# Softmax weights in a PSUM bank, more of the attention's additions open to GpSimd, and a new order, in a two-layer mixer kernel

## The chip, the cores and the metric

The kernel runs on one core of one Trainium2 chip. A core has five engines with queues of their own: TensorE (PE, matrix products; its weight loads are shown as PEld), VectorE (DVE), ScalarE (ACT), GpSimd (POOL) and SyncE (SP, which here issues the DMAs). They work side by side and wait for one another by semaphores. Data lie in SBUF (128 partitions), and matrix products land in PSUM, which this kernel uses as eight banks of 128 x 512 float32. The metric is device time in microseconds (us) of one execution; lower is better.

## The reference

x is 2048 rows of 512 float32. Two kinds of layers follow each other twice: x + A(layernorm(x)), then x + B(layernorm(x)). B (not touched by the change) is two layernorms, a spatial shift between two 512 x 512 products, and an MLP of 512 x 1792 and 1792 x 512 with gelu. A is attention with 32 heads of 16 numbers in which each row sees itself and seven earlier rows, two apart:

```python
idx = pos[:, None] - off[None, :]          # off = 0, 2, ..., 14
mask = idx >= 0
logits = jnp.einsum("bhsd,bhswd->bhsw", q, kg) * scale     # kg, vg: rows idx of k and v
logits = jnp.where(mask[None, None, :, :], logits, -1e9)
attn = _softmax(logits, axis=-1)
o = jnp.einsum("bhsw,bhswd->bhsd", attn, vg)
```

The kernel scales and shifts the logits by the maximum of the eight, takes exp, divides by the sum and adds up eight products for each output number. It must give these numbers whichever engine does a step.

## The kernel before, in words

The 2048 rows are cut into four blocks of 512 rows; with two layer pairs there are eight blocks n = 0 to 7. For each block the stages are: `p1_stream` (block 0: `p1_quarters`) normalizes x and makes q, k and v; `p2` is the attention; `p3` multiplies by wo, adds the residual and makes h; `p4` multiplies by w2; `p5` is the MLP (blocks 6 and 7 in the form `p5_pair`). Most products of float32 matrices are made as three products of float16 halves (high times high, high times low, low times high). So the normalizing steps end in `turn_dma` (lines 696 to 716): ACT rounds the high half, DVE or GpSimd subtracts it to get the low half, and a DMA transposes both (tiles `xt` and `nT`) for PE.

The attention of a block has two units, `p2_unit`, each for two quarters of the heads (U = 2; a quarter is 8 heads, 128 columns). In a unit:

- lines 1104 to 1113: for each quarter and each pair of row tiles, DVE multiplies windows of k by q into `prod` (128 x 2048) and sums 16 numbers at a time into the logits L (128 x 512 for the unit).
- lines 1127 to 1133: maximum over the eight window places, L minus maximum, exp on ACT, sum, reciprocal, L times reciprocal, all in SBUF and all on DVE but the exp.
- lines 1145 to 1161: for each quarter and pair of tiles, a product of V's windows with the weights into `prod` (2048 numbers a partition, 2 tiles x 8 window places x 128 columns), then a tree of three additions: `add4` (1024 sums), `add2` (512) and `add1` (256, into o). `add2` and `add1` may be made by DVE or GpSimd, `add4` by DVE.

Every step is an operation of a graph (`op`, with the helpers `dve`, `act`, `gp`, `pe`, `dma`). An operation has one or more alternatives, each with its engine and a planning cost in us. Two tables written out at the head of the file set what the program does: `PLACES` gives each operation, by its number, its place in the one order in which `plan` hands the operations out, and `OTHER` lists the numbers of operations that take their second alternative, the other engine. A class `InOrder` holds each engine's instructions in this order. The word "lock" on an alternative is a mark for the planner and is not used when the program runs.

Buffers are handed out by kind, in the same order, and come back when the last operation that touches them has been passed: `prod` has one buffer (`prod0` is a second one, for block 0 only), `L` two, `mm` four PSUM banks, `acc` four PSUM banks. All groups of matmuls but the sums over the MLP's width use `mm` banks: PE fills one with (mostly) twelve matmuls, and ACT or DVE empties it.

The profile puts nearly all instructions on one line (L335, the helper that issues them), so groups are told by their tiles: `prod<-kv,q` is the product with q (in block 0 some show x for q), `L<-prod` its sum, `prod<-kv,L` the product with the weights, `prod<-prod` the first two additions, `o<-prod` the last, `L<-L,mx` the subtraction of the maximum and the multiplication by 1/sum, `small` the one-number-a-partition statistics of the layernorms.

Of the kernel before, what the change touches and what calls it, by code (L numbers as in the profile page):

```python
# [12 lines left out]
ALU = mybir.AluOpType  # L13
# [4 lines left out]
P = 128  # L18
# [4 lines left out]
NT = 4  # L23
# [3 lines left out]
H8 = 8  # L27
DH = 16
W = 8
# [22 lines left out]
PE, DVE, ACT, POOL, SP = range(5)  # L52
# [268 lines left out]
def tile_mixer(ctx, tc, x_d, wqkv_d, wo_d, w1_d, w2_d, w3_d, w4_d, out_d):  # L321
# [73 lines left out]
    op = Graph()  # L395
# [82 lines left out]
    def dve(key, d, fn, r, w, lock=False, after=()):  # L478
        return op(key, [(DVE, d, fn, "lock" if lock else None)], r, w, after)
# [576 lines left out]
    def p2_unit(n, qts):  # L1056
        op.stage = ("p2_unit", n)
        l, b = lb[n]
        U = len(qts)
        L = Buf("L")  # L1060
        LW = NT * W * H8
# [552 lines left out]
```

## Time and profile before

| what | value |
|---|---|
| median of 3 runs | 1125.81 us (1124.1 to 1126.22) |
| the profiled execution | 1125.26 us |
| its span, from the first to the last instruction | 1123.5 us |
| granted TensorE clock | 0.999 |
| PE busy | 1105.1 us, 98% of the span |
| DVE busy | 935.1 us, 83% |
| ACT busy | 656.8 us, 58% |
| POOL busy | 496.1 us, 44% |

The page gives for each engine the time in which it was busy, the span in slices, the chain of work that ended last, and groups of instructions with their busy time, the mean duration of one in ns, and the idle time ahead of them with what ended it. A busy PE is not PE at its peak, since the ends of matmuls are modelled; idle time of an engine that is not the bottleneck costs nothing. Views of the trace give the same for any stretch of the span.

### The profile page before, as it was taken

The page shows a single profiled execution, that of the slowest core. Times are in us where ns is not written, and L with a number is a line of the kernel's source. Part 1 is how long each engine was busy: PE and PEld are TensorE (multiplying, and loading weights), DVE is VectorE, ACT ScalarE, POOL GpSimd, SP SyncE. Part 2 cuts the span into 40 slices and gives each one's busy share as a digit, 9 for nine tenths or more (in the row PEclk, how much of TensorE's full clock was granted, in tenths as well). Part 3 has the DMA queues.
Part 4 walks back from the last instruction along what each step waited for, and adds up shares of the span by engine and source line. Part 5 has one row for each costly group of instructions (what it writes and reads, how often), then busy time and mean ns, then how long its engine had stood idle before and what let it go on. Part 6 is the DMA issues. An engine that isn't in the chain of part 4 may idle for free.

```text
span 1123.5 us, 16172 instructions
## 1 busy us (share of the span) xinstructions
PE 1105.1 (98%) x5488; PEld 550.8 (49%) x5488; DVE 935.1 (83%) x1062; ACT 656.8 (58%) x1242; POOL 496.1 (44%) x583
## 2 busy tenths in 40 slices
PE   8999999999999999999999999999999999999998
PEld 6544444544444444444444444444444447455764
DVE  5999999989899789879999899789887999746431
ACT  4976885358853577366655566464555654466341
POOL 4658584336531453123535345335524357333231
PEclk9999999999999999999999999999999999999999
DMA  8789999989998579946798859995889759556642
GB/s 219 193 228 223 235 267 244 265 229 230 240 241 215 127 186 209 239 125 166 172 241 201 207 126 248 248 236 164 200 211 240 198 138 251 147 155 130 186 136 61
DMA packets 268995, 224.00 MB, mean 199 GB/s; under 512 B 143688, under 2 KB 205128, under 8 KB 268912
## 3 DMA queue, kind: packets, MB, share of 16 engines
q1 hardware_dynamic: 267296, 221.20, 78.7%
q10 hardware_dynamic: 1616, 1.77, 0.6%
q8 instruction: 43, 0.70, 0.3%
q14 instruction: 40, 0.33, 0.1%
HBM read 143.65 MB, written 41.54 MB: 165 GB/s over the span
## 4 chain that ended last, share of the span: by engine, by line
PE 78%; DVE 8%; DMA 4%; POOL 3%; ACT 2%; issue 2%; SPq 1%; POOLq 0%; DVEq 0%; ACTq 0%
PE mm L335 55%; PE acc L335 23%; DVE prod L335 4%; DVE L L335 1%; POOL small L335 1%; DMA w<-in_B_w_dram 1%; SPq L335 1%; DMA out_dram<-x 1%; POOL f L335 1%; DMA w<-w 1%; ACT junk L335 0%; DVE mx L335 0%; POOL prod L335 0%; DMA xt<-f 0%; ACT f L335 0%
## 5 line engine op out<-in xcount | busy, mean ns | idle before, releaser
L335 PE MATMUL acc<-w,g 128*128 128x512 f16 (+1 forms) x1092 | 268.0, 396 | 1.4 <-DMA w<-in_B_w_dram 0.7
L335 PE MATMUL mm<-nT,w 128*128 128x512 f16 (+2 forms) x1176 | 235.8, 354 | 2.7 <-DMA nT<-f 2.7
L335 PE MATMUL mm<-wq_hl,xt 128*128 128x512 f16 x1008 | 225.3, 379 | 4.5 <-DMA xt<-f 4.0
L335 PEld LDWEIGHTS <-w 128*128 128x128 f16 x1464 | 139.5, 98 | 121.7 <-issue 6.7
L335 PEld LDWEIGHTS <-g 128*128 128x128 f16 x1176 | 114.7, 98 | 136.5 <-DVE g L335 2.1
L335 PEld LDWEIGHTS <-xt 128*128 128x128 f16 x1008 | 98.3, 98 | 122.8 <-DMA xt<-f 5.2
L335 DVE TENSOR_TENSOR prod<-kv,L 128x2048 f32<-128x2048 f32 x64 | 151.3, 2364 | 3.1 <-POOL o L335 2.1
L335 DVE TENSOR_REDUCE L<-prod 128x128 f32<-128x2048 f32 x64 | 146.1, 2283 | 1.1
L335 ACT ACTIVATE mm<-mm,s_w 128x512 f32<-128x512 f32 (+1 forms) x109 | 70.0, 645 | 117.1 <-PE mm L335 116.7
L335 DVE TENSOR_TENSOR prod<-kv,q 128x2048 f32<-128x2048 f32 x58 | 135.1, 2329 | 2.2 <-POOL o L335 0.8
L335 DVE TENSOR_TENSOR prod<-prod 128x512 f32<-128x512 f32 (+1 forms) x115 | 120.4, 1048 | 3.1
L335 POOL TENSOR_TENSOR small<-small,nhalf 128x1 f32<-128x1 f32 (+1 forms) x104 | 87.3, 842 | 64.5 <-ACT small L335 60.3
L335 POOL TENSOR_SCALAR small<-small 128x1 f32<-128x1 f32 (+1 forms) x129 | 68.5, 533 | 66.8 <-ACT junk L335 31.7
L335 POOL TENSOR_TENSOR g<-f,g 128x512 f16<-128x512 f32 x35 | 45.9, 1315 | 94.2 <-ACT f L335 49.8
L335 PE MATMUL mm<-w_hl,h 128*128 128x512 f16 x384 | 86.0, 379 | 0.0
L335 PE MATMUL mm<-nT,w_hl 128*128 128x512 f16 x384 | 85.8, 379 | 0.0
L335 PE MATMUL mm<-wo_hl,oT 128*128 128x512 f16 x336 | 74.2, 379 | 0.0
L335 ACT ACTIVATE ev<-mm,s_kv 128x512 f32<-128x512 f32 x56 | 38.0, 681 | 52.5 <-PE mm L335 32.1
L335 PEld LDWEIGHTS <-oT 128*128 128x128 f16 x426 | 41.7, 98 | 49.3
L335 POOL TENSOR_TENSOR o<-prod 128x256 f32<-128x256 f32 x26 | 22.7, 872 | 83.6 <-DVE prod L335 74.0
L335 PEld LDWEIGHTS <-w_hl 128*128 128x128 f16 x384 | 37.5, 98 | 44.9 <-issue 0.5
L335 PEld LDWEIGHTS <-h 128*128 128x128 f16 x384 | 37.6, 98 | 44.6
(250 smaller groups left out, 1585.6 us busy)
## 6 DMA issues: line engine op xcount, KB each, us to landing
w<-w SPq DMA_DIRECT2D x183, 256.0 KB
kv<-kv_d SPq DMA_DIRECT2D x112, 352.0 KB
w<-in_B_w_dram SPq DMA_DIRECT2D x56, 256.0 KB
kv_d<-ev SPq DMA_DIRECT2D x112, 128.0 KB
q_d<-ev SPq DMA_DIRECT2D x28, 256.0 KB
w<-g SPq DMA_DIRECT2D x28, 256.0 KB
q<-q_d SPq DMA_DIRECT2D x28, 256.0 KB
x<-x SPq DMA_DIRECT2D x27, 256.0 KB
```

The costliest lines, as they stand in the source:

```text
L335: i = f(*a, **k).ins
```

## The change

Three things are changed.

First, the weights (exp times 1/sum) are no longer written back into L in SBUF. The multiplication writes them to a new buffer `Lm` of kind "mm", a PSUM bank (512 float32 for the two quarters of a unit), and the four products with V of the unit read them there. These products lose their planner's mark "lock".

Second, `add4` and the subtraction of the maximum get a second alternative on GpSimd, as `add2` and `add1` had before. All handle two row tiles at a time, as before.

Third, `PLACES` and `OTHER` are written anew: another order of all 3807 operations, and 366 operations instead of 333 on their second alternative.

```diff
+        Lm = Buf("mm")
+        Lmv = lambda u: Lm.t[:, LW * u:LW * (u + 1)].rearrange("p (h t j) -> p t j h", t=NT, j=W)
...
-        dve(kd, t2, lambda: V.tensor_sub(L4(), L4(), wide(mx)), [mx], [all_L], lock=True)
+        op(kd, [(DVE, t2, lambda: V.tensor_sub(L4(), L4(), wide(mx)), "lock"),
+                (POOL, 1.95 * t2, lambda: G.tensor_sub(L4(), L4(), wide(mx)), None)], [mx], [all_L])
...
-        dve(kd, t2, lambda: V.tensor_mul(L4(), L4(), wide(sm)), [sm], [all_L], lock=True)
+        dve(kd, t2, lambda: V.tensor_mul(Lm.t[:, :U * LW].rearrange("p (h t j) -> p h t j", t=NT, j=W), L4(), wide(sm)),
+            [sm, all_L], [Lm], lock=True)
...
                 dve(kd + 0.02, 2.29, lambda i=i, pv4=pv4, kv=kv, u=u: V.tensor_tensor(
                     pv4().rearrange("p t j (h d) -> p t j h d", d=DH), win_h(kv[1].t, i, 2),
-                    Lv(u)[:, i:i + 2].unsqueeze(4).to_broadcast([P, 2, W, H8, DH]), ALU.mult),
-                    [all_L, *kv_in[1]], [pr, (o, 9)], lock=True)
+                    Lmv(u)[:, i:i + 2].unsqueeze(4).to_broadcast([P, 2, W, H8, DH]), ALU.mult),
+                    [Lm, *kv_in[1]], [pr, (o, 9)])
...
-                dve(kd + 0.01, 1.215, lambda f=add4: f(V), [], [pr], lock=True)
+                op(kd + 0.01, [(DVE, 1.215, lambda f=add4: f(V), "lock"), (POOL, 2.45, lambda f=add4: f(G), None)], [], [pr])
```

In the new order the multiplication by 1/sum of the two units of block 3 stands at places 1447 and 1615, and the last of their four products at 1661 and 1687. Between 1615 and 1661 stand PE's groups into "mm" at 1619, 1627, 1637, 1646, 1653 and 1658 and one group into "acc" at 1657, DVE's product at 1644, and at 1648 the DVE instruction that empties the bank of the group of 1637.

348 rows, old and new, of tables (OTHER, PLACES) are left out of this document.

## The prediction, written before the changed kernel ran

> **What bounds the kernel now.** I read the span first, then busy time by stage (the view of windows: busy time, instructions in brackets, then clock and DMA share), then what TensorE waited for, then the chain of waits inside the stage in which it waited.
>
> ```profile
> span 1123.5 us, 16172 instructions
> ```
> ```profile
> 0.00:25.00 25.00, 21.72 (x118) 17.17 (x119) 11.75 (x34) 10.19 (x28) 10.94 (x38) 1.00 0.87 218
> 25.00:75.00 50.00, 49.98 (x196) 26.57 (x195) 49.19 (x47) 43.06 (x107) 27.52 (x29) 1.00 0.77 206
> 75.00:200.00 125.00, 116.35 (x556) 55.92 (x555) 118.66 (x132) 88.29 (x173) 89.44 (x79) 1.00 0.97 241
> 200.00:925.00 725.00, 724.10 (x3316) 330.78 (x3315) 644.89 (x678) 425.70 (x783) 298.96 (x347) 1.00 0.83 204
> 925.00:1000.00 75.00, 73.85 (x472) 45.71 (x471) 57.77 (x75) 36.12 (x62) 35.07 (x38) 1.00 0.76 204
> 1000.00:1123.50 123.50, 119.11 (x837) 74.61 (x835) 52.87 (x100) 53.47 (x95) 34.18 (x54) 0.99 0.45 122
> ```
>
> The columns after the length are PE, PEld, DVE, ACT and POOL. PE is the bound almost everywhere: from 200 to 925 us it is idle for 725.00 - 724.10 = 0.9 us, while DVE has 80 us to spare there. The change removes no matmul, so what can be won is PE's idle time: 3.3 us at the start (nothing has arrived yet), 8.65 us from 75 to 200, 0.9, then 1.15 from 925 to 1000, and 4.4 in the last stretch (the last tiles' additions and stores after the last matmul). Start and end stay. That leaves 8.65 + 0.9 + 1.15 = 10.7 us, 1% of the span, as the most that any relief of the other engines can give. Four fifths of it lie where DVE is busy 118.66 of 125 us. PE's own waits:
>
> ```profile
> PE mm L335 <- DMA xt<-f: 4.0, 4, 1.4
> PE mm L335 <- DMA nT<-f: 2.7, 1, 2.7
> PE mm L335 <- DVE f L335: 2.2, 2, 1.4
> PE mm L335 <- ACT f L335: 1.1, 1, 1.1
> PE acc L335 <- DVE g L335: 1.1, 2, 1.0
> ...
> PE mm L335 <- DVE h L335: 0.4, 1, 0.4
> PE mm L335 <- ACT ev L335: 0.2, 1, 0.2
> ```
>
> The first two are waits for transposed tiles that the normalizing steps deliver. The last two are all that PE ever waits for a PSUM bank to be emptied: 0.6 us with four "mm" banks. Behind one of the four waits on xt (chain of waits, 103 to 120 us):
>
> ```profile
> 104.38 2.97 POOL small L335 x2
> 107.35 0.08 issue
> 107.44 3.36 POOL small L335
> ...
> 115.23 4.29 DMA xt<-f
> ```
> ```profile
> 105.32 5.74 POOL L335 TENSOR_SCALAR small<-small 128x1 f32<-128x1 f32 x3
> ```
> ```profile
> 104.96 2.29 DVE L335 TENSOR_TENSOR prod<-kv,L 128x2048 f32<-128x2048 f32 x1
> 107.29 1.22 DVE L335 TENSOR_TENSOR prod<-prod 128x1024 f32<-128x1024 f32 x1
> 108.43 2.28 DVE L335 TENSOR_TENSOR prod<-kv,L 128x2048 f32<-128x2048 f32 x1
> ```
>
> Three GpSimd instructions of one number a partition take 5.74 us, because DVE runs products of V with the weights (prod<-kv,L) beside them. With DVE on an instruction that has one operand in PSUM, this does not happen:
>
> ```profile
> 1044.05 0.42 DVE L335 TENSOR_TENSOR f<-mm,ev 128x256 f32<-128x256 f32 x1
> ```
> ```profile
> 1044.02 0.73 POOL L335 TENSOR_TENSOR f<-f,ev 128x256 f32<-128x256 f32 x1 [2.22 <-DVE f L335]
> ```
>
> There GpSimd's addition started 0.03 us before DVE's and neither held the other.
>
> **The change, part by part.**
>
> ```profile
> L335 DVE TENSOR_TENSOR prod<-kv,L 128x2048 f32<-128x2048 f32 x64 | 151.3, 2364 | 3.1 <-POOL o L335 2.1
> ...
> L335 DVE TENSOR_TENSOR prod<-prod 128x1024 f32<-128x1024 f32 x64 | 84.0, 1313 | 1.7
> L335 DVE TENSOR_TENSOR prod<-prod 128x512 f32<-128x512 f32 x51 | 36.5, 715 | 1.4
> ```
> ```profile
> L335 POOL TENSOR_TENSOR prod<-prod 128x512 f32<-128x512 f32 x14 | 20.2, 1446 | 50.8 <-DVE prod L335 50.8
> ...
> L335 POOL TENSOR_TENSOR w_hl<-nT,w_hl 128x1024 f16<-128x1024 f32 x1 | 2.1, 2138 | 0.1
> ```
>
> 1. Weights in PSUM. The 16 multiplications by 1/sum write an "mm" bank, and the 64 products read it. An operand in PSUM is priced by
>
> ```profile
> L335 DVE TENSOR_TENSOR f<-mm,ev 128x512 f32<-128x512 f32 x11 | 7.5, 683 | 12.0 <-issue 4.8 <-ACT ev L335 3.9 <-PE mm L335 3.3
> ...
> L335 DVE TENSOR_TENSOR x<-x,f 128x512 f32<-128x512 f32 x9 | 6.2, 683 | 0.1
> ```
>
> 683 ns from PSUM and 683 ns from SBUF: no price. An unhindered product took 2.28 (above) against a mean of 2.364, so up to 64 x 0.08 = 5 us of DVE time may go; writing to PSUM instead of SBUF has no row of its own, and I bound it between 0 and 0.1 us a piece (16 of them, 1.6 us), and take 0. The Trainium skill's page "VectorE: DVE Perf Modes", section "The TRN2 errata", speaks against this: its table gives a PSUM source 62 cycles more at 0.96 GHz, by which the products would take 64 x 0.065 = 4.2 us more (an estimate), a half microsecond of it among the eight products between 75 and 200 us. The two rows of 683 ns do not show it.
>
> 2. GpSimd gets more. The list OTHER names the operations that take their second engine. Counted in the order in which the program makes them: of the 64 first additions (128x1024) 8 go to GpSimd, of the 16 subtractions of the maximum 5, of the 64 second additions 18 where 13 went, of the last additions 27 where 26 went; of the 28 low halves for xt 19 where 14 went; of the residual additions 10 where 14 went. With the rows of 512 elements for subtractions, second additions and low halves, and 0.4 us on DVE and 1.1 on GpSimd for a last addition (256 elements, an estimate that continues the rows of 1024 and 512), DVE loses 8 x 1.313 + 15 x 0.715 + 0.4 = 21.6 us and gets 4 x 0.683 = 2.7 back: 19 us net. GpSimd gets 8 x 2.14 + 15 x 1.45 + 1.1 - 4 x 1.45 = 34 us. An addition of 1024 elements on GpSimd is not in the trace in this form; the row of 2138 ns has two inputs of that length and is the nearest; below it is bounded by DVE's 1.31, above by 2 x 1.446 = 2.9, which includes being held by DVE. Added wait: prod is one buffer (two in block 0), so the next product on DVE stands behind a first addition on GpSimd and the two steps after it, and whatever follows the product in DVE's queue waits too. Eight times up to 2.14 - 1.31 = 0.8 us more is 6.6 us of DVE idle at worst. From 200 to 925 DVE's 80 idle us hide it; three of the eight lie in block 0, where a second product buffer is the cover, and would cost DVE 2.5 us without it.
>
> 3. Order. PLACES is written anew. PE's sequence is nearly the old one; SP issues the same transfers, none more.
>
> What PE gains, by its waits. The wait ahead of 119.57 us loses 5 us of its chain (5.74 against about 0.75 for three free instructions) but is itself only some 0.9 us long: -0.9, after which the transfer of 4.29 us is late next. Of the other three waits on xt (3.1 us) I take away not quite half, because GpSimd now makes two more of the low halves that feed them and DVE has less ahead of them: -1.4. Of the 2.7 on nT a third: -0.9; its chain is longer and ends in a transfer. In the stage from 925 to 1000 this row of the chain of waits lies ahead of PE:
>
> ```profile
> 964.09 1.13 DVE g L335
> ```
>
> It stands behind a product with V that held GpSimd; I take half of the 1.15 us: -0.6. For the lent bank I add 0.5, about as much again as today's 0.6. Sum: -0.9 - 1.4 - 0.9 - 0.6 + 0.5 = -3.3 us. The profiled execution took 1125.26 us by the clock of the runs (span 1123.5), the median of the three runs 1125.81, 0.05% above it. Forecast: **1122.0 us**.
>
> **Rivals.**
>
> *DMA is what PE waits for.* From 75 to 200 us the 16 DMA engines are busy 0.97 of the time, and the waits on xt and nT end in transfers of 4.29 us and more. An earlier subtraction then only queues earlier. The terms on xt and nT vanish (3.2 us of the 3.3), the bank's 0.5 and the 0.6 cancel: 1125.2. Against it: ahead of the transfer the chain spends 6.3 us in GpSimd alone.
>
> *The lent bank stops PE (slower).* A bank is held from the multiplication by 1/sum to the last of four products. In block 3 the new places of two such units overlap: 1447 to 1661 and 1615 to 1687, so between 1615 and 1661 two banks are left, and PE has six groups that write "mm" there (1619, 1627, 1637, 1646, 1653, 1658) with one acc group among them. Today the same groups run back to back with all banks:
>
> ```profile
> 427.94 13.11 PE L335 MATMUL mm<-wq_hl,xt 128*128 128x512 f16 x60
> 440.89 10.52 PE L335 MATMUL mm<-nT,w 128*128 128x512 f16 x48
> ```
>
> Nine groups of twelve matmuls, 2.59 us each. The group at 1653 needs the bank that DVE empties at 1648, right behind a product at 1644: if DVE lags by one product, PE stands for 2.3 to 3 us. It decides once two or three such stalls occur over the 16 units: at half a microsecond for each unit (8 us) the time is 1125.3 - 3.8 + 8 = 1129.5. The Trainium skill's page "PSUM — Partial Sum Buffer", section "Summary: rules for kernel authors", says the same in four words, "Evacuate promptly"; no row shows what a bank held for tens of microseconds does here. For it: PE has no slack at all from 200 to 925, each stall counts in full. Against it: bank waits are 0.6 us today.
>
> *The port is not freed.* If the products go on holding GpSimd, the added 34 us of GpSimd work meet the old locks, and additions of 2.14 us hold DVE in turn: term one goes, waits grow by one or two, 1126.5. The pair of rows at 1044 us speaks against it.
>
> **How the numbers follow.** A measurement of this kernel can tell about 0.2%, 2.3 us, from no change. The forecast with its neighbours (1118 to 1123.5) gets 0.50, DMA 0.25, the bank 0.20, the port 0.05, of which I count 0.03 as the same and 0.02 as slower. So faster 0.50, same 0.28, slower 0.22. The lower end takes two thirds of the 10.7 us, with the bank free: 1117.5. The upper end takes in the bank's case: 1130.
>
> **What would show it.** Right: GpSimd's small instructions under prod<-kv products keep 0.2 to 0.6 us; the mean of those products falls to 2.28 to 2.30; idle PE from 75 to 200 falls to some 5.5 us; PE's waits on ACT and DVE that empty banks stay under 1.5 us in all. Wrong: idle PE of several microseconds between 200 and 925, released by ACT ev or by DVE g, h, x or f (the bank); idle PE from 75 to 200 as before, released by DMA (the first rival); small GpSimd instructions of 2 us beside prod<-kv products (the port).

## The result, and the profile after

The changed kernel takes 1140.72 us (median of 4 runs, 1135.84 to 1143.46) against 1126.01 of the kernel before (4 runs, 1124.1 to 1129.2): ratio 1.0125, 95% interval 1.0109 to 1.0142. It is slower, and outside the range that was forecast (1117.5 to 1130). The profiled execution took 1138.72 us. Of all executions told of here one, of the version with four units below, ran at a granted clock of 0.655 and took 1669.28 us; no ratio counts it.

The page's span and busy times, then the view of windows for three of the same stages as before, for PE alone (length, PE busy and its instructions, clock, DMA share, GB/s):

```profile
span 1136.9 us, 16149 instructions
...
PE 1108.8 (98%) x5488; PEld 551.1 (48%) x5488; DVE 907.6 (80%) x1023; ACT 646.9 (57%) x1219; POOL 505.5 (44%) x643
```
```profile
25.00:75.00 50.00, 44.45 (x170) 0.93 0.68 184
75.00:200.00 125.00, 118.04 (x560) 1.00 0.95 235
200.00:925.00 725.00, 717.55 (x3280) 1.00 0.82 203
```

DVE lost 27 us of work, as the change meant it to, and PE's idle time rose from 18.4 us (1123.5 - 1105.1) to 28.1. By stage: 25 to 75 us from 0.02 to 5.55, 75 to 200 from 8.65 down to 6.96, 200 to 925 from 0.9 to 7.45. PE's work itself is 3.7 us longer; the clock row of the first stage shows half of that (below). What PE waited for:

```profile
PE mm L337 <- ACT x L337: 5.5, 2, 5.3
PE mm L337 <- ACT junk L337: 3.9, 3, 2.0
PE mm L337 <- ACT ev L337: 3.5, 4, 1.8
PE mm L337 <- DMA nT<-f: 2.3, 3, 1.1
PE acc L337 <- POOL g L337: 1.5, 2, 0.9
PE mm L337 <- DVE f L337: 1.5, 1, 1.5
```

`ACT x` and `ACT ev` empty banks: 9.0 us where `ACT ev` had 0.2. The longest wait, at 50.19 us, stands before the first bank is lent (the first multiplication that writes one starts at 63.3 us). Three timelines of the changed kernel, of ACT, GpSimd and DVE, show how it came about (start, length, instruction, and in brackets the idle time ahead of it and its releaser):

```profile
41.67 1.89 ACT L337 ACTIVATE wo_hl<-nT 128x2048 bf16<-128x2048 f32 x1
...
43.56 0.86 ACT L337 ACTIVATE x<-mm,small 128x128 f32<-128x128 f32 x3
48.98 0.29 ACT L337 ACTIVATE small<-small 128x1 f32<-128x1 f32 x1 [4.56 <-POOL small L337]
...
49.27 1.64 ACT L337 ACTIVATE x<-mm,small 128x128 f32<-128x128 f32 x6
```
```profile
44.59 2.48 POOL L337 TENSOR_TENSOR small<-small,nhalf 128x1 f32<-128x1 f32 x1
47.05 1.90 POOL L337 TENSOR_SCALAR small<-small 128x1 f32<-128x1 f32 x1
```
```profile
44.38 4.48 DVE L337 TENSOR_TENSOR prod<-kv,x 128x2048 f32<-128x2048 f32 x2
```

ACT stands 4.56 us behind a statistic of one number that GpSimd delivers late (DVE's products of K, in the last of the three, hold it; the change does not touch them), and behind that statistic wait the instructions that empty two banks. In the kernel before GpSimd made that statistic itself: the new list of second engines put it on ACT, ahead of the emptying. And the product with its weights in PSUM:

```profile
L337 DVE TENSOR_TENSOR prod<-kv,mm 128x2048 f32<-128x2048 f32 x64 | 146.0, 2284 | 9.8 <-POOL o L337 6.1 <-DMA kv<-kv_d 2.2 <-DMA kv<-kv 0.6
```

2284 ns, against 2364 before. So one half of the reasoning held at once. What cost more was open: the lent bank, the new order, or GpSimd's longer list. The waits bound the first of these. The rows in which a bank is emptied (`ACT x`, `ACT ev`, and of the smaller ones `DVE prod` with 0.7 us and `DVE g` with 0.3) add up to 10.0 us; 5.5 of them end before any bank is lent, so at most 4.5 us can be PE's own waits for the lent banks.

### The profile page after: what moved, and what is told of

It reads as the page before. It is cut to its first block, busy times and chain, and to the rows that moved or that the text cites. A ratio compares the mean times of both kernels' runs of the same rounds, so it can differ in the third digit from the quotient of the medians.

```text
span 1136.9 us, 16149 instructions
## 1 busy us (share of the span) xinstructions
PE 1108.8 (98%) x5488; PEld 551.1 (48%) x5488; DVE 907.6 (80%) x1023; ACT 646.9 (57%) x1219; POOL 505.5 (44%) x643
## 4 chain that ended last, share of the span: by engine, by line
PE 55%; DVE 8%; DMA 3%; ACT 2%; issue 2%; POOL 2%; SPq 1%; DVEq 0%; POOLq 0%; ACTq 0%
PE mm L337 38%; PE acc L337 17%; DVE prod L337 4%; DVE f L337 1%; DMA w<-in_B_w_dram 1%; DVE g L337 1%; DMA kv<-kv_d 1%; ACT f L337 1%; DMA nT<-f 1%; DVE L L337 1%; POOL small L337 1%; SPq L337 1%; ACT g L337 0%; POOL prod L337 0%; DMA w<-g 0%
## 5 line engine op out<-in xcount | busy, mean ns | idle before, releaser
L337 PE MATMUL acc<-w,g 128*128 128x512 f16 (+1 forms) x1128 | 277.0, 395 | 1.7 <-POOL g L337 1.5
L337 DVE TENSOR_TENSOR prod<-kv,mm 128x2048 f32<-128x2048 f32 x64 | 146.0, 2284 | 9.8 <-POOL o L337 6.1
L337 DVE TENSOR_TENSOR prod<-prod 128x512 f32<-128x512 f32 (+1 forms) x104 | 103.9, 1000 | 4.5 <-POOL prod L337 1.8
L337 POOL TENSOR_TENSOR small<-small,nhalf 128x1 f32<-128x1 f32 (+1 forms) x104 | 76.4, 737 | 58.2 <-ACT small L337 54.7
L337 POOL TENSOR_TENSOR g<-f,g 128x512 f16<-128x512 f32 x33 | 43.0, 1306 | 83.9 <-ACT g L337 57.3
L337 POOL TENSOR_TENSOR prod<-prod 128x512 f32<-128x512 f32 (+2 forms) x29 | 46.8, 1613 | 49.4 <-DVE prod L337 47.6
L337 PEld LDWEIGHTS <-w_hl 128*128 128x128 f16 x384 | 37.5, 98 | 45.9 <-issue 1.3
```

The costliest lines, as they stand in the source:

```text
L337: i = f(*a, **k).ins
```

## The experiments

Four theories: **bank** (PE and DVE stop for the lent banks), **order** (the new places and the new list of second engines cost), **GpSimd** (its longer additions hold up `prod`), and, on the side of the gain, **port** (what it is worth that the products leave GpSimd free). The runs undo or do one part at a time, in both orders.

Each ratio is to the kernel before on the same chip (1125.6 to 1126.4 us there). "Port held" means that the products read both operands in SBUF and hold GpSimd; "port free" that they read the weights in PSUM.

### The lent bank in the old order

**Part one alone.** The code of the change with the tables PLACES and OTHER of the kernel before. Every engine has its old order; where the multiplication finds no bank free, it is put later in the one order, up to the point where one is.

```diff
-PLACES, OTHER of the changed kernel
+PLACES, OTHER of the kernel before (192 operations at another place, no engine's order changed)
```

> Part one alone: the weights stand in an mm bank, while every engine keeps the order of the kernel before and its list of second engines (all first additions and subtractions as before). 192 operations change their place in the one order, none its place on its engine; only the hand-out of banks differs. Theory 'order': the lent bank costs little and the freed port wins something, 1121 to 1127 (ratio 0.996 to 1.001), idle PE from 200 to 925 under 2.5 us. Theory 'bank': idle PE from 200 to 925 grows from 0.9 to 5 us or more, released by the instructions of ScalarE and VectorE that empty banks, 1130 or more. Both expect the product of V with the weights at 2.28 to 2.29 us and GpSimd's small instructions under it at 0.2 to 0.6 us.

1183.99 us, ratio 1.0525 (1.0501 to 1.0549). PE's waits, and below them DVE's timeline at 213 us:

```profile
PE mm L335 <- ACT ev L335: 9.5, 10, 2.4
PE mm L335 <- DVE h L335: 9.2, 4, 3.0
PE mm L335 <- DVE prod L335: 7.1, 4, 2.3
PE mm L335 <- ACT g L335: 6.8, 6, 2.0
```
```profile
213.24 2.29 DVE L335 TENSOR_TENSOR prod<-kv,q 128x2048 f32<-128x2048 f32 x1
228.63 0.70 DVE L335 TENSOR_TENSOR mm<-L,mx 128x512 f32<-128x512 f32 x1 [13.10 <-ACT g L335]
```

Idle PE from 200 to 925 us is 725.00 - 687.54 = 37.5 us. The second fence is a wait that the prediction didn't list: the multiplication itself needs a bank, and DVE stood 13.1 us before it, with everything behind it in its queue. Theory "order" falls in the form in which it was put: in the old order the lent bank costs 58 us.

**Bank only.** Is it the missing bank, or the operand in PSUM? The same hand-out, but nothing is written to the bank.

```diff
-        dve(kd, t2, lambda: V.tensor_mul(Lm..., L4(), wide(sm)), [sm, all_L], [Lm], lock=True)
+        dve(kd, t2, lambda: V.tensor_mul(L4(), L4(), wide(sm)), [sm], [all_L, Lm], lock=True)
...
-                    Lmv(u)[:, i:i + 2]..., [Lm, *kv_in[1]], [pr, (o, 9)])
+                    Lv(u)[:, i:i + 2]..., [all_L, Lm, *kv_in[1]], [pr, (o, 9)])
```

> The order of the kernel before; a bank is lent from the multiplication by 1/sum to the last of the four products, exactly as in the run of part one alone, but nothing is written to it: the weights stay in SBUF and the products go on holding GpSimd. Theory 'bank': the 58 us of part one alone are the lent bank's, and without the free port the kernel is as slow or slower, 1184 to 1200. Theory 'operand in PSUM' (the loss comes from writing or reading the weights in PSUM, not from the missing bank): 1124 to 1130.

1169.8 us, 1.0398 (1.0374 to 1.0422): between the two forecasts. Three quarters of the 58 us come with nothing in PSUM at all. The remainder could be the port or a fault of this experiment: since nothing touches the bank, neither does the multiplication wait for it, nor PE for the product.

**True hold.** One number is written into the bank and copied out behind each product.

```diff
+            V.tensor_copy(Lm.t[:, :1], flat(sm)[:, :1])
...
+                    V.tensor_copy(spare, Lm.t[:, :1])
```

> The run 'bank only' again, with a lent bank that is truly in use: the multiplication by 1/sum also writes one number a partition into it, and each product is followed by a copy of that number out of it (80 very small instructions more on VectorE, some 8 us, most of them off PE's path), so that the multiplication must wait for a free bank and PE's next group in that bank must wait for the product. In 'bank only' nothing touched the bank, so only the rotation among the other banks changed (1170 against 1126). The weights stay in SBUF, GpSimd is held as before. Theory 'wait' (the 14 us between 1170 and the 1184 of part one alone are these two waits): 1178 to 1192, with VectorE waiting some 13 us for a bank ahead of a multiplication. Theory 'operand' (they come from the operand in PSUM or from the freed port): 1168 to 1175.

1190.34 us, 1.0575 (1.0551 to 1.06). Of DVE's waits:

```profile
DVE mm L335 <- ACT g L335: 12.5, 1, 12.5
```

It stands where part one alone had the 13.1 us. Theory "wait" holds: a lent bank that is really used costs 64 us in the old order, and freeing the port takes 6 of them back (1190.3 to 1184.0). The 80 small copies are in both numbers; DVE is busy for 942.2 us with them, 7 us more than in the kernel before.

**Short holds.** In 14 of the 16 units the multiplication is cut by quarters, each piece with a bank of its own right ahead of its products (the code is shortened to these units).

```diff
-        Lm = Buf("mm")
...
         for u, qt, kd, kv, kv_in in part_of:
+            Lm, hs8 = Buf("mm"), slice(H8 * u, H8 * (u + 1))
+            dve(kd, 0.425, lambda Lm=Lm, hs8=hs8: V.tensor_mul(
+                Lm.t[:, :LW].rearrange("p (h t j) -> p h t j", t=NT, j=W), L4()[:, hs8],
+                hv(sm)[:, hs8].unsqueeze(3).to_broadcast([P, H8, NT, W])), [sm, all_L], [Lm], lock=True)
```

> Part one in the order of the kernel before, but with the multiplication by 1/sum cut into two, one for each quarter of the heads, each with a bank of its own and placed right ahead of the first product that reads it (in 14 of the 16 units), so that a bank is lent for some 21 us in two pieces instead of 29 us in one. 14 multiplications more of 0.43 us on VectorE, two of 0.43 instead of one of 0.69: under 3 us, off PE's path. Theory 'slack': in the trace of before, summing over all fillings of an mm bank that start while a bank would be lent what is missing to 2.6 us (one group of twelve matmuls) of slack between the emptying of the bank and its filling gives 51.6 us, near the 58 us measured; with the shorter holds the same sum is 28.4 us, so 58 falls to about 32: 1150 to 1165. Theory 'any lent bank breaks the order' (what counts is that one is lent, not how long): 1175 or more.

1182.89 us, 1.0514 (1.0495 to 1.0533): no gain, the theory "slack" is refuted as a formula. PE's waits on the products doubled:

```profile
PE mm L337 <- DVE prod L337: 14.3, 6, 5.0
PE mm L337 <- DVE h L337: 11.3, 2, 9.4
```

and DVE waited for a bank for

```profile
DVE mm L337 <- ACT g L337: 15.8, 2, 10.8
...
DVE mm L337 <- ACT ev L337: 4.2, 1, 4.2
...
DVE mm L337 <- ACT f L337: 2.5, 1, 2.5
```

22.5 us in all (13.1 + 2.5 in part one alone); it now takes one 30 times instead of 16. PE's waits on `ACT ev` did fall, from 9.5 us to 4.0, but what the shorter hold spared came back in these two places.

### The new order, without and with what it was made for

**Weights in SBUF.** The changed kernel with this one part undone.

```diff
-        dve(kd, t2, lambda: V.tensor_mul(Lm..., L4(), wide(sm)), [sm, all_L], [Lm], lock=True)
+        dve(kd, t2, lambda: V.tensor_mul(L4(), L4(), wide(sm)), [sm], [all_L], lock=True)
...
-                    Lmv(u)[:, i:i + 2]..., [Lm, *kv_in[1]], [pr, (o, 9)])
+                    Lv(u)[:, i:i + 2]..., [all_L, *kv_in[1]], [pr, (o, 9)])
```

> The changed kernel with the weights back in SBUF (the multiplication writes L, the products read L), order and list of second engines of the changed kernel kept. Four banks are free for PE again, and the products hold GpSimd again. Theory 'bank': most of the loss goes, 1128 to 1132, and the waits at 443 us (2.0 us) and 446 us vanish. Theory 'order': the early wait of 5.3 us stays, the other losses stay or grow with the port, 1138 to 1145; of the bank at most the 2 to 3 us at 443 us come back.

1166.12 us, 1.0359 (1.0335 to 1.0383): more than either theory gave. From the page:

```profile
PE 1119.2 (96%) x5488; PEld 552.2 (47%) x5488; DVE 934.0 (80%) x1023; ACT 647.0 (56%) x1219; POOL 596.4 (51%) x643
```

GpSimd needs 596 us for the work that takes it 506 in the changed kernel, because DVE's products hold it.

**True hold in the new order.** The bank lent, the port held: the two small copies above, with the tables of the changed kernel.

> The same true hold in the order and with the list of second engines of the changed kernel: the bank is lent as there, the weights stay in SBUF, and the products hold GpSimd. Against the changed kernel (1141) only the port is taken away, against the new order with weights in SBUF (1166) only the bank is lent. Theory 'port' (the new order has paid for the banks with other places, and lives on the free port): 1162 to 1172, 25 us over the changed kernel and within 6 us of the run without a lent bank. Theory 'bank' (lent banks cost much in this order too): 1176 or more.

1169.82 us, 1.0388 (1.0365 to 1.041). With it the table is full (medians in us):

| | no bank lent, port held | bank lent, port held | bank lent, port free |
|---|---|---|---|
| old order | 1126.0 (before) | 1190.3 | 1184.0 |
| new order | 1166.1 | 1169.8 | 1140.7 (the change) |

The middle column has the small copies in it. In the new order the lent bank costs 4 us instead of 64 (by the two medians; the intervals, 1.0335 to 1.0383 and 1.0365 to 1.041, overlap), and the free port is worth 29 instead of 6; but the new order alone, its places and its second engines with the port held, costs 40.

**New places, old engines.** The weights in SBUF and OTHER of the kernel before; only the places are new.

> The new order with weights in SBUF, and each operation on the engine that it had before (list of second engines of the kernel before): no bank lent, no port freed, no first addition on GpSimd; only the places differ from the kernel before. Theory 'GpSimd's longer list' (the 40 us of the new order with weights in SBUF come from 34 us more work on a GpSimd that the products hold): 1130 to 1145. Theory 'order' (the places themselves cost): 1155 or more.

1221.62 us, 1.0849 (1.0829 to 1.0869). So the 40 us are not GpSimd's longer list as such: the new places cost 96 us with the old engines and 40 with the new ones. The old places with the new engines were not run.

### Parts of the changed kernel

**Additions and subtractions on DVE.** The 13 operations taken out of OTHER.

> The changed kernel with the eight first additions and the five subtractions of the maximum that went to GpSimd back on VectorE; everything else as changed. Theory 'GpSimd' (an addition of 2.35 us on GpSimd holds prod, and with it VectorE and what VectorE empties): 1134 or less, with fewer waits of PE on VectorE and on GpSimd. Theory 'order' and theory 'bank': 1138 to 1143, within 2 us of the changed kernel, since VectorE has 105 us to spare from 200 to 925 us either way.

1138.45 us, 1.0116 (1.0091 to 1.0141), which is not told apart from the changed kernel's 1.0125 (1.0109 to 1.0142). Theory "GpSimd" falls for the additions and subtractions taken back; GpSimd's other new work was not taken back alone.

**Block 3 in SBUF.** The block named in the prediction.

```diff
+        if n != 3:
             dve(kd, t2, lambda: V.tensor_mul(Lm...
+        else:
+            Lm, Lmv = L, Lv
+            dve(kd, t2, lambda: V.tensor_mul(L4(), L4(), wide(sm)), [sm], [all_L], lock=True)
```

> The changed kernel, its order kept, with block 3 alone keeping its weights in SBUF: the two units of block 3 lend no bank (they held one for 65 and 31 us), and its eight products hold GpSimd again. Theory 'the named place' (the overlap of two lent banks in block 3 is a main part of the loss): PE's waits of 2.0 us at 443 us and 1.1 us at 446 us go, 1136 to 1138. Theory 'spread' (the new order has paid for the banks everywhere, and the port is what it lives on): the waits at 443 us go, but as much or more comes back as waits on what GpSimd delivers between 395 and 480 us, 1139 to 1146.

1146.72 us, 1.0184 (1.0169 to 1.02): 6 us slower. First the timeline of PE in the changed kernel, then in this one:

```profile
435.63 5.34 PE L337 MATMUL mm<-wq_hl,xt 128*128 128x512 f16 x24
442.80 2.75 PE L337 MATMUL mm<-wq_hl,xt 128*128 128x512 f16 x12 [1.83 <-ACT ev L337]
446.45 3.83 PE L337 MATMUL mm<-nT,w 128*128 128x512 f16 x17 [0.91 <-DMA nT<-f]
```
```profile
438.64 7.93 PE L337 MATMUL mm<-wq_hl,xt 128*128 128x512 f16 x36
452.18 4.42 PE L337 MATMUL mm<-nT,w 128*128 128x512 f16 x10 [5.61 <-DMA nT<-f]
```

The bank's wait at 443 us is gone, and the next wait, for a tile that GpSimd's steps feed, grew from 0.91 to 5.61 us. One of these steps, a subtraction of 128x512 on GpSimd, took 2.66 us beside a product that now reads SBUF; in the changed kernel it took 1.16. So a bank did stop PE in the named overlap, but giving it back costs more in the port. The stop was not at the named group, though. Counted in groups of twelve matmuls, the wait at 442.80 us is that of the group at place 1619, for a bank that ACT empties. The group at 1653, which was to stand behind DVE, follows without a wait; DVE had emptied its bank 0.3 us before (`DVE g`, 453.25 us, 0.75 long):

```profile
454.33 2.75 PE L337 MATMUL mm<-nT,w 128*128 128x512 f16 x12
```

**Short holds in the new order.** The cut by quarters, on the changed kernel.

> The changed kernel with the same cut of the multiplication into quarters (15 of the 16 units), order otherwise as changed. Theory 'slack': what the new order still loses to lent banks comes back, at most the 2.0 us at 443 us and about 2.5 us in smaller waits: 1135 to 1139. Theory 'order' (the rest of the loss lies in waits on transfers, GpSimd and ScalarE that no bank sets): within 2 us of the changed kernel, 1138 to 1143.

1145.04 us (1141.0 to 1152.01), 1.0175 (1.013 to 1.022): above both forecasts, and no gain is shown here either.

**Banks emptied first.** The early fault of the order mended.

```diff
-497 515 84 85 ... 93
+84 85 93 497 515 ...
```

(Numbers of operations in the one order: 497 and 515 are the statistics, 84 a group of matmuls, 85 and 93 the emptying.)

> The changed kernel with one edit of its order: two of ScalarE's instructions that empty an mm bank in the first 55 us (x<-mm,small at places 166 and 171) stand ahead of two one-number statistics that wait for GpSimd (places 163 and 164). No bank is lent to the weights before some 57 us, so this stall is not the lent bank's. Theory 'order' (the new order queues instructions that empty banks behind statistics that wait for GpSimd): PE's wait of 5.3 us at 45 us falls under 1 us, the six matmuls behind it run at full rate again (1.75 us), granted clock of 25 to 75 us back to 1.00, time 7 us under the changed kernel: 1133 to 1135. Theory 'bank' (the loss comes from the lent banks in the attention of all blocks): the wait goes, too, but most of the 13.4 us of span stay: 1133 or more. Third possibility, the wait is cover for a later wait on transfers: less than 2 us won, 1139.

1138.19 us, 1.0128 (1.0091 to 1.0166). The wait of 5.3 us is gone (0.4 left on `ACT x`), and the time is not told apart from the changed kernel's: 2.25 us came back at 52.55 us as a wait for the first transposed tile, which stands behind the same statistics, and 1.64 us at 71.58 behind another statistic.

**Five faults mended.** The same, and four small matmuls with their next steps placed one group later.

> The changed kernel with five faults of its order mended: the two emptying instructions ahead of the statistics (as in the first run), and four small matmuls that sum the squares of weights (they waited 1.8, 1.5, 0.9 and 0.7 us for ScalarE in that run), each with its two or three following steps, one group of matmuls later. Theory 'single faults': 3 to 5 us under the run with one fault mended (1138.2), 1133 to 1136. Theory 'the next input is late': PE waits for the next group instead, within 1.5 us of 1138.

1142.04 us, 1.0144 (1.0127 to 1.0162). Nothing won: theory "single faults" falls. Which input is late at each place of the new order stays open; mending one wait brought out another.

### Weights in PSUM where a bank lies idle

**Six units.** In the old order, the 6 of 16 units in which a bank (five times one of acc, once one of mm) can be lent without another hand-out moving.

```diff
+LENT_OF = {(0, 0): 'acc', (1, 0): 'acc', (1, 2): 'acc', (2, 0): 'acc', (3, 2): 'acc', (4, 2): 'mm'}
...
-        Lm = Buf("mm")
+        kind = LENT_OF.get((n, qts[0]))
+        Lm = Buf(kind)
```

> Order and engines of the kernel before; the weights stand in PSUM in 6 of the 16 units only: those where a bank can be lent in the old order without any later hand-out changing place (the first unit of block 0, both of block 1, the first of block 2 and the second of block 3 take one of the four acc banks, the second of block 4 an mm bank). 24 of the 64 products leave GpSimd free. Theory 'bank' (it is the missing mm bank that costs, not the weights in PSUM): 1121 to 1126, no loss, and GpSimd's small instructions under these products at 0.2 to 0.6 us. If weights in PSUM cost by themselves, or lending breaks the order even where the bank lies idle: 1130 or more.

1141.46 us, 1.014 (1.0117 to 1.0164). The loss is in two places, of which this is the larger (PE's timeline):

```profile
450.63 2.11 PE L336 MATMUL acc<-w,g 128*128 128x512 f16 x9
461.66 1.44 PE L336 MATMUL acc<-w,g 128*128 128x512 f16 x3 [8.92 <-DVE prod L336]
```

One bank lent once, and PE stood 8.92 us for the last product (it starts at 459.33 us and takes 2.27): the hand-out had not moved, but the times had no room.

**Four units.** Without those two.

> As the run that lends idle banks, without the two units in which PE waited for the lent bank (9.1 us for an acc bank at 462 us, 2.4 us for an mm bank at 599 us, and 3.5 us at half clock behind them). Four units are left: the first of block 0, both of block 1, the first of block 2, each with an acc bank. Theory 'bank': nothing is lost any more, 1123 to 1126.5. The prediction's gains by the port would show as up to 2 us, in idle PE from 75 to 200 us (8.65 us before). If weights in PSUM cost by themselves: 1128 or more.

1126.23 us, 0.9996 (0.9987 to 1.0005). In these four units the weights in PSUM cost nothing by themselves, and the freed port wins nothing that can be told.

**Five units.** And the second unit of block 0, in which the prediction saw its first gain.

> The four units and, with an mm bank, the second unit of block 0, under whose products GpSimd's three small instructions took 5.74 us before. The prediction took 0.9 us off PE's wait ahead of 119.57 us for it. Theory 'port is worth the predicted term': 0.5 to 1 us under the run with four units. Theory 'bank': PE waits there for the product that holds the mm bank, as it did for 2.4 us at 121 us in the run of part one alone: 1 to 3 us over the run with four units.

1126.19 us, 1.0001 (0.9992 to 1.0009). GpSimd's small instructions, and PE's wait at the place of the old one ahead of 119.57 us:

```profile
104.16 1.14 POOL L336 TENSOR_SCALAR small<-small 128x1 f32<-128x1 f32 x3
```
```profile
119.02 5.34 PE L336 MATMUL mm<-wq_hl,xt 128*128 128x512 f16 x24 [1.08 <-DVE prod L336]
```

Three instructions that took 5.74 us take 1.14 (0.2 to 0.6 each was forecast); PE still waits a microsecond there, now for the lent bank. Neither four nor five units beat the kernel before, and no other version did.

## Why the prediction was wrong, step by step

- **The bound.** Right. PE is the bound in every run, and what the runs differ by is mostly its waits and the half clock behind them.
- **Weights in PSUM at no price.** Right: 2284 ns a product (2280 to 2300 forecast), and four units at 0.9996. The 4.2 us (an estimate) that the Trainium skill's table ("VectorE: DVE Perf Modes", "The TRN2 errata") would add did not show. The multiplication into PSUM took 0.70 us in the median, as an unhindered subtraction of the same shape into SBUF (0.70 at 54.02 us in the kernel before).
- **GpSimd gets more.** Sized nearly right: an addition of 1024 took 2.36 us (2.14 taken, bounds 1.31 to 2.9), DVE has 27 us less (19 and up to 5 forecast), and the wait that was added behind a first or second addition is

```profile
DVE prod L337 <- POOL prod L337: 4.7, 2, 2.9
```

  4.7 us. With DVE's waits behind last additions (`DVE prod <- POOL o`, 2.9 us before and 6.1 after) and those of its own last additions (`DVE o <- POOL prod`, 3.8 and 0.9) it is 5.0 us more in all, under the 6.6 that were the worst case. The run with these operations on DVE shows none of it on PE's path.
- **The port is freed.** Right as a mechanism (the rival "not freed" falls): 1.14 us for 5.74. But the terms drawn from it (-0.9, -1.4, -0.9, -0.6) did not show in the old order, as far as it was tried: four units in blocks 0 to 2 give 0.0 with 0.1% either way, and a fifth, the unit of the first -0.9, adds nothing. The -0.6, which belongs to a later block, was not tried there. In the stage from 75 to 200 us the changed kernel did win 1.7 us, of 3.2 forecast. The rival "DMA" (1125.2) had these terms at nothing; the runs don't show that a transfer was the reason. If the port is held in the new order, as the rival "not freed" had it at 1126.5, the time is 1169.8: that rival priced the lock, but not how much of the new order rests on the free port.
- **"For the lent bank I add 0.5, about as much again as today's 0.6."** This step failed in size. In the order for which the 0.6 us was measured a lent bank costs 64 us; in the new order, for which the term was meant, 4 us by two medians, and at most 4.5 by PE's own waits for banks. That PE seldom waits for one of four banks says nothing of what it does with three: the 0.6 us was a planned result, not a margin. The rival "the lent bank stops PE" had the mechanism and the sign, but its 8 us came from the places of one block; and it missed that DVE waits for a bank as well (13.1 us in one piece in the old order, 1.5 us in all in the changed kernel).
- **"PE's sequence is nearly the old one."** This step failed too, and it weighs most: the new order got no price, and this sentence was the only reason given. By the two tables 209 of PE's 497 operations keep their rank among PE's and 455 stay within three ranks, so the sentence is roughly true and beside the point. The new order lowers the bank's cost from 64 to 4 us, and takes 40 for it, of which the free port gives 29 back: 1126.0 + 40.1 + 3.7 - 29.1 = 1140.7, a sum that closes by the way it is made, since each run undoes one part more. A part of an order's price lies in how the other engines' instructions stand to PE's: a statistic of one number ahead of an emptying made PE wait 5.3 us, and the wait went when the emptying was put first with PE's order as it was. But the time did not fall with it, so why the order costs 40 us stays open in the main.
- **What would show it.** The sign that was named for the bank came by half. PE is idle for 7.45 us from 200 to 925, where 0.9 had been, but a bank is emptied in only two of the rows behind it:

```profile
PE mm L337 <- DMA nT<-f: 2.3, 3, 1.1
PE mm L337 <- ACT ev L337: 1.8, 1, 1.8
PE acc L337 <- POOL g L337: 1.5, 2, 0.9
PE mm L337 <- DVE mx L337: 0.9, 1, 0.9
PE mm L337 <- ACT junk L337: 0.4, 1, 0.4
PE mm L337 <- DVE g L337: 0.3, 1, 0.3
```

  These are `ACT ev`, the 1.8 us in the named overlap of block 3, and `DVE g` with 0.3. The rest waits for tiles and statistics, which no sign had in it for this stage. Over the whole span PE waits 10.0 us for banks to be emptied where under 1.5 was named as the sign of being right, but more than half of that stands ahead of the first lent bank. Mending five places of the order did not lower the time.
- **The range.** Its lower end is off by its own working: two thirds of the 10.7 us below 1125.26 are 1118.1, not 1117.5. The measured time lies at the other end.

The trace of before did hold a warning, seen when the program's order of operations is laid on the trace. Between the emptying of an mm bank and its next filling lay 4.1 us in the median; of the 139 fillings that start while a bank would be lent, 46 had less than the 2.6 us of one group, and what they lack adds up to 51.6 us. As a formula it failed (short holds should have won 26 us and won 1); as a bound it would have spoken of tens of microseconds, not of half of one. The same sum on the trace of the new order with the weights in SBUF is 18.9 us (20 of 138 fillings): smaller, as the bank's cost there is, but far above it.

## What to carry to other kernels

Before a buffer of a tightly ordered pipeline is lent, look at how long each copy lies empty between two uses, not at how seldom the bound engine waits for one, and count the borrower's own wait for it. When an order is rewritten together with a change, the order is a part of the change with a price of its own: run the change in the old order and the new order without the change, since here one cost 58 us and the other 40 while both together cost 15. Look, too, for waits that came before the changed part can act: here the longest one did. In an order that runs late in many places, one wait mended is worth only what the next one leaves of it: nothing here, for one place and for five.

## What the runs showed of the hardware

**A short wait can cost PE its clock.** The view of windows of the changed kernel, PE alone, around the wait of 5.3 us:

```profile
44.50:46.90 2.40, 0.35 (x2) 0.99 0.01 3
46.90:53.70 6.80, 3.51 (x6) 0.50 0.44 101
53.70:60.00 6.30, 6.30 (x26) 1.00 0.72 201
```

Six matmuls ran at half the granted clock after the wait had ended, 1.75 us more (half of 3.51). Over 16 profiles, each of the 26 waits of PE over 3.05 us had a stretch at clock 0.50 (3.4, 6.8 or 10.2 us long) that began in the wait or less than 2 us after it; of the 56 between 2.05 and 3.05 us 31 had one, of the 34 between 1.5 and 2.05 one, a wait of 1.80 us. The Trainium skill ("TensorE: Matmul & The Clock Gate", "Part 1: The HAM clock gate (the "warmup" mystery)") has a window of about 3.4 us that runs free, and half clock after one idle window: the lengths agree, but here waits of 2.05 us, and once one of 1.80, were followed by the half clock. In the run of part one alone PE was busy for 1121.2 us instead of 1105.1; by half of PE's busy time in these stretches some 11 of the 16 us are the clock.

**GpSimd can be passed over by several of DVE's instructions.** An instruction of one number a partition, and DVE beside it, in the changed kernel:

```profile
35.65 5.45 POOL L337 TENSOR_SCALAR small<-small 128x1 f32<-128x1 f32 x1
```
```profile
36.05 1.01 DVE L337 SCALAR_TENSOR_TENSOR wq_hl<-nT,inv_q,wq_hl 128x384 f16<-128x384 f32 x2
36.99 4.06 DVE L337 SCALAR_TENSOR_TENSOR wq_hl<-h,inv_q,wq_hl 128x1152 f16<-128x1152 f32 x3
```

It ended when five instructions of DVE, back to back and all with two operands in SBUF, had ended. The Trainium skill ("SBUF — State Buffer", "SBUF: two separate sides") tells of a lock for the length of one instruction; here GpSimd was held through five. This is one place, and not the rule: in the timelines of the result GpSimd's statistic at 44.59 us ended at 47.07, some 0.4 us behind the first of DVE's two products (4.48 us from 44.38 on for both), while the second was running. What decides this is not shown.
